# Channel taps computed during the start, half of unit 1's stores issued by GpSimd, and unit 2's conv jobs begun four steps earlier

## The chip, the cores and the metric

The kernel runs on one core of a Trainium2 chip. The metric is the device time of one execution in microseconds; the time before is the median of three runs, 773.52 us (773.24 to 773.58). A core has five engines that run side by side, each with an instruction queue of its own that is worked in order: TensorE (PE, matmuls; PEld are its weight loads), VectorE (DVE), ScalarE (ACT), GpSimd (POOL) and SyncE (SP, which here only issues DMAs). They wait for one another by semaphores. DMAs are issued by SyncE or by GpSimd and land later. GpSimd's DMAs can change the type on the way (float32 to float16), and SyncE's can transpose.

## What is computed

A lightweight convolution is followed by a gated feed-forward block. The reference, cut to what matters:

```python
# x: (8, 4096, 192), weight: (8 heads, 7 taps); 192 channels = 8 heads x 24
w = exp(weight - max) ; w = w / (sum(w) + 1e-9)          # softmax over the 7 taps
x_pad = concatenate([zeros(6 rows), x])                  # causal, for each sequence
out[b, s, head, :] = sum_k w[head, k] * x_pad[b, s + k, head, :]
x = out.reshape(32768, 192)                              # tokens
g = x @ w_gate ; val = x @ w_val                         # (192, 1536) each
result = (g / (1 + exp(-g)) * val) @ w_out               # (1536, 192), float32
```

## The kernel before

**Tiling.** The 32768 tokens are 64 blocks of 512 (`TB`), and four blocks make a unit (`UB`), so there are 16 units. A step `n` is one block and one of 12 slices of 128 hidden columns: 768 steps in all, `b, j = divmod(n, 12)`. In a step, `gate_val(n)` makes six matmuls of 512 columns (three slices of 64 channels, for gate and for val side by side, line 846), ScalarE the silu (L855) and VectorE the product `h` (L857). The down projection is done for three steps at a time: in each step with `j % 3 == 1`, `slot` and `down` issue 24 matmuls into the accumulators (L872), and its first one waits for the silu of two steps before. So the work has a period of three steps. When a block's sums are ready, ScalarE and VectorE copy them out (L929, L930) and SyncE stores them (L933). The order of the instructions on each engine is the order in which the code calls `seq`.

**Four ways to the convolved, transposed input.** Blocks 0 to 3 (unit 0) go through `early` or `early_pair`, matmuls with a banded matrix, and are transposed on TensorE by `eturn` (L490 the transposes, L501 the copies out of the bank) or, for block 3, through DRAM. Unit 1 (blocks 4 to 7) goes through `conv_half` (steps 25 and 31): matmuls L531, copies to `tm` (L548), one copy by GpSimd (`conv_dup`, L559), then nine stores to DRAM (`conv_out`, L567 and L575, all by SyncE, called at steps 31 and 32), then transposing loads (`fetch`, L589, three for each block, at steps 32, 35, 38 and 41). Units 2 to 15 (`POOLED`) are convolved element by element: GpSimd casts x into DRAM (`cast_x`, L649), SyncE loads it transposed (`turn_x`, L665) and joins a half tile to another (`join_x`, L669), and a conv job for each of six tiles of a unit multiplies by the seven channel taps: ScalarE tap 0 and two more (L742), VectorE two (L717), GpSimd two and the sums (L707, L692). `place` (L766) then puts the tiles together.

**What sets the order.** `planned(v)` gives the steps at which unit v's head, cast, turns, joins and jobs are called; `queue_jobs` puts six jobs into two lists (`act_steps`, `dve_steps`), and `pooled_work` takes from them one ScalarE and one VectorE piece in the steps with j = 1, 4, 7 and 10 (ScalarE; two in every other j = 10) and j = 1, 7 and 10 (VectorE). Unit 2's jobs are called at step 38, its first join at step 36.

**The channel taps.** A job needs, for each of 128 channels, the seven taps of its head (`both_taps`). They are made from the softmaxed weights `split` by a matmul with a 0/1 matrix of heads by channels (`pick`). GpSimd prepares `which` and `above` for it at the start (L210, L218, behind the loads of the weights), VectorE makes `pick` at step 34 (L609), and at step 37 TensorE makes four small matmuls (L620) into a gate bank and ScalarE copies them out (L627).

**The start.** GpSimd issues, in this order: block 0's x, the first third of gate and val weights (`load_w(0)`), the second third, block 1's x, the last third, `w_out` in thirds, and x for blocks 2 and 3 and for unit 1. Meanwhile the taps are spread to a banded matrix (`make_wide`, L344, with `ident` L352 for the transposes), then `early(0)` convolves block 0 (L386, copies L404 and L413), `eturn(0)` transposes it, and step 0 begins.

PSUM has three banks for gate, three for val and two accumulators; each new tile of a tag takes the next bank in turn and waits until the last reader of that bank is done.

## Time and profile before

| what | us or share |
|---|---|
| median of three runs | 773.52 (773.24 to 773.58) |
| the profiled execution: its own time | 772.68 |
| its span, and the rest around it | 770.9 and 1.8 |
| granted TensorE clock, mean over the span | 0.999 |
| step 0's first gate matmul starts | 8.78 |
| step 767's first gate matmul starts | 763.75 |
| a conv piece on ScalarE (L742), VectorE (L717), mean | 0.71, 1.07 |
| a sum on GpSimd (L692, total with part), mean | 1.28 |
| first conv piece on GpSimd starts, idle time ahead of it | 60.97, 20.6 |

The profile is of one execution. Busy shares say how much of the span an engine worked; the chain that ended last says which work the end of the run followed from; the list of waits says who waited for whom, and the timeline gives the instructions of a stretch in the order of time: start, duration, engine, line, operation, `out<-in`, shape, count, and in brackets the idle time of the engine before it with what ended it. Successive matmuls overlap, so that the pace is read from their starts, not from their durations. A row of several instructions ("x3") begins with the first of them and gives the time from its start to the last one's end.

### The profile page before, as it was taken

What the parts mean: (1) busy time and instruction counts of PE and PEld (TensorE: products, weight loads), DVE (VectorE), ACT (ScalarE), POOL (GpSimd) and SP (SyncE); (2) the same over time, 40 slices, a digit from 0 to 9 for tenths busy, and PEclk for the clock granted to TensorE, in tenths of its full rate; (3) what the DMA queues carried; (4) which work ended last, traced back from release to release, by engine and by line L of the source; (5) the groups of instructions that cost most, each with busy time, mean ns of one, the idle gap of its engine ahead of it and who ended that gap; (6) DMA issues with size and microseconds to landing.
All of it is one profiled execution on the core that took longest, in us unless ns stands there. A gap on an engine that the chain in (4) does not pass through costs nothing.

```text
span 770.9 us, 27696 instructions
## 1 busy us (share of the span) xinstructions
PE 764.5 (99%) x11041; PEld 673.9 (87%) x11041; DVE 697.3 (90%) x1042; ACT 645.1 (84%) x1107; POOL 618.1 (80%) x557
## 2 busy tenths in 40 slices
PE   8999999999999999999999999999999999999997
PEld 5766688888888888999999999999999999999997
DVE  7778999999999999999999999999999999999775
ACT  6678888888888888888888888888888888888664
POOL 9105889999989898998989989999899998889300
PEclk9999999999999999999999999999999999999999
DMA  9968746653545444456443444336454443221211
GB/s 138 190 131 136 143 77 154 128 87 90 117 85 125 102 86 106 99 99 116 85 107 93 93 118 108 92 84 116 92 118 100 84 116 90 55 67 40 70 57 43
DMA packets 140898, 77.78 MB, mean 101 GB/s; under 512 B 84632, under 2 KB 137632, under 8 KB 140768
## 3 DMA queue, kind: packets, MB, share of 16 engines
q1 hardware_dynamic: 127824, 60.24, 34.3%
q0 software_dynamic: 12944, 15.77, 13.4%
q8 instruction: 86, 1.41, 0.7%
q14 instruction: 44, 0.36, 0.2%
HBM read 31.54 MB, written 37.58 MB: 90 GB/s over the span
## 4 chain that ended last, share of the span: by engine, by line
PE 97%; SPq 1%; ACT 0%; DMA 0%; issue 0%; DVE 0%; ACTq 0%
PE gate L846 32%; PE val L846 32%; PE acc L872 31%; SPq L589 1%; PE warm L946 0%; PE turn L490 0%; SPq L567 0%; PE acc L893 0%; DMA x<-x 0%; PE cv L531 0%; PE cv L386 0%; PE cv L429 0%; ACT tme L404 0%; DVE h L857 0%; ACT wide L344 0%
## 5 line engine op out<-in xcount | busy, mean ns | idle before, releaser
L857 DVE TENSOR_TENSOR h<-sig,val 128x512 f16<-128x512 f16 x768 | 497.6, 683 | 65.5 <-PE gate L846 48.9
L855 ACT ACTIVATE sig<-gate 128x512 f16<-128x512 f32 x768 | 457.5, 597 | 110.4 <-PE gate L846 71.9
L846 PE MATMUL gate<-pxc,w 64*128 64x512 f16 x2016 | 471.2, 376 | 0.0
L846 PE MATMUL val<-pxc,w 64*128 64x512 f16 x2016 | 471.1, 376 | 0.0
L846 PEld LDWEIGHTS <-w 64*128 64x128 f16 x4608 | 397.4, 110 | 65.2 <-issue 1.1
L872 PE MATMUL acc<-wo,h 64*128 64x192 f16 x6096 | 319.2, 243 | 0.2
L872 PEld LDWEIGHTS <-h 64*128 64x128 f16 x6096 | 301.3, 94 | 19.3 <-ACT sig L855 1.1
L692 POOL TENSOR_TENSOR total<-total,part 128x512 f32<-128x512 f32 x168 | 214.1, 1275 | 70.3 <-DVE total L717 50.5
L717 DVE SCALAR_TENSOR_TENSOR total<-x,both_taps,total 128x512 f32<-128x512 f16 x168 | 179.4, 1068 | 0.0
L707 POOL TENSOR_SCALAR piece<-x,both_taps 128x512 f32<-128x512 f16 x168 | 154.5, 920 | 0.0
L692 POOL TENSOR_TENSOR total<-total,piece 128x512 f32<-128x512 f32 x84 | 119.1, 1417 | 7.0
L742 ACT ACTIVATE part<-x,both_taps 128x512 f32<-128x512 f16 x168 | 120.0, 715 | 0.0
L692 POOL TENSOR_TENSOR pxc<-total,piece 128x512 f16<-128x512 f32 x56 | 71.6, 1279 | 4.7
L846 PE MATMUL val<-xc,w 64*128 64x512 f16 x288 | 68.5, 376 | 0.0
L846 PE MATMUL gate<-xc,w 64*128 64x512 f16 x288 | 68.2, 377 | 0.0
L742 ACT ACTIVATE total<-x,both_taps 128x512 f32<-128x512 f16 x84 | 60.0, 714 | 1.2 <-DMA x<-x 1.2
L692 POOL TENSOR_TENSOR y<-total,piece 128x512 f16<-128x512 f32 x28 | 35.6, 1273 | 2.3
L930 DVE COPY o_sb<-acc 128x384 f32<-128x384 f32 x63 | 34.6, 549 | 0.0
L929 ACT COPY o_sb<-acc 128x384 f32<-128x384 f32 x63 | 29.7, 471 | 3.3 <-PE acc L872 3.3
L559 POOL COPY tm<-tm 128x1280 f16<-128x1280 f16 x1 | 1.3, 1251 | 17.4 <-DVE tm L548 17.4
L649 POOL DMA_DIRECT2D xs<-in_x_dram x14 | 8.5, 606 | 0.0
L946 PE MATMUL warm<-fill 128*128 128x512 f16 (+1 forms) x12 | 4.2, 510 | 1.0 <-DVE fill L92 1.0
(73 smaller groups left out, 65.1 us busy)
## 6 DMA issues: line engine op xcount, KB each, us to landing
out_dram<-o_sb SPq DMA_DIRECT2D x63, 384.0 KB
pxc<-pxc SPq DMA_DIRECT2D x112, 64.0 KB
pxc<-y SPq DMA_DIRECT2D x112, 64.0 KB
xs<-in_x_dram POOLq DMA_DIRECT2D x7, 774.0 KB, 6.8
xs<-in_x_dram POOLq DMA_DIRECT2D x7, 768.0 KB, 6.7
x<-in_x_dram POOLq DMA_DIRECT2D x4, 480.0 KB, 11.0
x<-x SPq DMA_DIRECT2D x28, 66.0 KB
x<-xs SPq DMA_TRANSPOSE x112
```

Of the source, the lines that this page charges most:

```text
L589: nc.sync.dma_start_transpose(out=t[:, 0:TB], in_=scr[u][TB * i : TB * i + TB, Q * k : Q * k + P])
L649: nc.gpsimd.dma_start(out=flat[skip * D : rows * D].rearrange("(a n) -> a n", n=n), in_=bass.AP(tensor=x_flat.tensor, offset=(u * UT - XP ...
L692: nc.gpsimd.tensor_tensor(job["dst"] if k == K - 1 else total, total, part, op=ALU.add)
L707: nc.gpsimd.tensor_scalar(part, shifted(k), scalar1=job["tap"][:, k : k + 1], scalar2=1.0, op0=ALU.mult, op1=ALU.mult,)
L717: nc.vector.scalar_tensor_tensor(job["total"], shifted(k), job["tap"][:, k : k + 1], job["total"], op0=ALU.mult, op1=ALU.add,)
L742: nc.scalar.activation(part, shifted(k), AF.Copy, scale=job["tap"][:, k : k + 1])
L846: nc.tensor.matmul(o, w16[m][p0 : p0 + Q, k, e::E], xc[b][k][p0 : p0 + Q, 0:TB], start=(k == 0), stop=(k == SL - 1),)
L855: silu[n] = seq(nc.scalar.activation(sg, g, AF.Silu)).ins
L857: seq(nc.vector.tensor_tensor(hj, sg, v, op=ALU.mult))
L872: nc.tensor.matmul(acc[b][bank][:, s, :], hj[p0 : p0 + Q, ts(2 * bank + s, P)], wo16[p0 : p0 + Q, j, :], start=(not second and j == 0 and ...
L929: seq(nc.scalar.copy(o_sb[:, 0:2, :], acc[b][0]))
L930: seq(nc.vector.tensor_copy(o_sb[:, 2:4, :], acc[b][1]))
```

## The change

The index rows that `pick` is made from become one row of head numbers (`head_of`), which GpSimd writes between the first and the second third of the weights; two such rows and two compares behind `w_out` go. `make_picks` now compares `head_of` with the partition number in one instruction for all 192 channels and one for the last 64 again, and is called between `make_wide` and `early(0)`. `make_channel_taps` is called inside `eturn(0)`, behind its transposes, and takes a val bank; the copy out (`copy_channel_taps`) is called behind `eturn(0)`'s copies. Of unit 1's eight numbered stores, 1, 3, 5 and 7 are issued by GpSimd; the ninth, the rest of store 7, stays with SyncE. Unit 2's first join moves from step 36 to step 32, where it follows block 4's three transposing loads and precedes block 5's; its jobs are called at step 34 instead of 38, so that the first ScalarE piece is in step 37 instead of 40. Otherwise the order on SyncE's queue stays as it was; on GpSimd's, unit 3's cast (called at step 56) comes behind the second conv job's pieces instead of ahead of them.

```diff
--- before.py
+++ after.py
@@ -196,26 +196,18 @@
     cid = small("cid", [P, P], i32)
     seq(nc.gpsimd.iota(cid, pattern=[[1, P]], base=0, channel_multiplier=0))
     load_w(0)
+    head_of = small("head_of", [H, D], i32)
+    seq(
+        nc.gpsimd.iota(
+            head_of, pattern=[[1, H], [0, grp]], base=0, channel_multiplier=0
+        )
+    )
     load_w(1)
     xe_tile(1)
     xe_load(1)
     load_w(2)
     for m in range(3):
         load_wo(m)
-    which = {}
-    above = {}
-    for name, first, rows in (("c01", 0, P), ("c2", P, Q)):
-        which[name] = small(f"which_{name}", [H, P], i32)
-        seq(
-            nc.gpsimd.iota(
-                which[name],
-                pattern=[[0, P // rows], [1, rows]],
-                base=first,
-                channel_multiplier=-grp,
-            )
-        )
-        above[name] = small(f"above_{name}", [H, P])
-        seq(nc.gpsimd.tensor_single_scalar(above[name], which[name], 0, op=ALU.is_ge))
     xp = cpool.tile([P, 2 * EG, D], fp16, tag="xp", name="xp", bufs=1)
     for r in range(2):
         windows(xp, Q * r, (2 + r) * TB, EO, 0, 2 * EG)
@@ -476,7 +468,7 @@
             )
             xc[b].append(t)
 
-    def eturn(b, where):
+    def eturn(b, where, then=None):
         tiles = [
             cpool.tile([P, XW], fp16, tag=f"xc{k}", name=f"xc{k}", bufs=8)
             for k in range(SL)
@@ -491,6 +483,8 @@
                         bank[:, g, :], tme[b][:, g, Q * k : Q * k + P], ident
                     )
                 )
+        if then is not None:
+            then()
         whole = ((dve, 0, 0, 0, 0, P), (act, 1, 0, 1, 0, P), (dve, 2, 0, 2, 0, P))
         halves = (
             (dve, 0, 0, 0, 0, P), (act, 2, 0, 2, 0, P),
@@ -508,6 +502,8 @@
                 )
             )
         xc[b] = tiles
+        if b == 0:
+            copy_channel_taps()
 
     tm = {}
     scr = {}
@@ -560,11 +556,12 @@
 
     def conv_out(u, m):
         r, c = divmod(m, 4)
+        queue = nc.gpsimd if m % 2 else nc.sync
         t0 = NG * CO * m
         full = min(NG, (UT - t0) // CO)
         rest = min(UT - t0 - full * CO, CO) if full < NG else 0
         seq(
-            nc.sync.dma_start(
+            queue.dma_start(
                 out=scr[u][t0 : t0 + full * CO, :].rearrange("(g j) d -> j g d", j=CO),
                 in_=tm[u][32 * c : 32 * c + CO, NG * r : NG * r + full, :],
             )
@@ -603,17 +600,21 @@
     pick = {}
 
     def make_picks():
-        for name in which:
-            pick[name] = small(f"pick_{name}", [H, P], fp16)
-            seq(
-                nc.vector.scalar_tensor_tensor(
-                    pick[name], which[name], float(grp), above[name],
-                    op0=ALU.is_lt, op1=ALU.mult,
-                )
-            )
+        picks = small("picks", [H, 2 * P], fp16)
+        for c0, c1, to in ((0, D, 0), (P, D, D)):
+            seq(
+                nc.vector.tensor_scalar(
+                    picks[:, to : to + c1 - c0], head_of[:, c0:c1], scalar1=pf[0:H],
+                    scalar2=None, op0=ALU.is_equal,
+                )
+            )
+        pick.update(c01=picks[:, 0:P], c2=picks[:, P : 2 * P])
+
+    tap_bank = []
 
     def make_channel_taps():
-        bank = ppool.tile([P, TB], fp32, tag="gate", name="ctap")
+        bank = ppool.tile([P, TB], fp32, tag="val", name="ctap")
+        tap_bank.append(bank)
         for m, name in enumerate(pick):
             for a in range(2):
                 seq(
@@ -623,8 +624,10 @@
                         skip_group_check=True,
                     )
                 )
+
+    def copy_channel_taps():
         both_taps = small("both_taps", [P, 2 * K])
-        seq(nc.scalar.copy(both_taps, bank[:, 0 : 2 * K]))
+        seq(nc.scalar.copy(both_taps, tap_bank[0][:, 0 : 2 * K]))
         for m, name in enumerate(pick):
             taps[name] = both_taps[:, m * K : m * K + K]
 
@@ -785,11 +788,11 @@
             (0, 0), (0, Q), (1, Q), (1, 0), None, (2, 0), (2, Q), (3, Q), (3, 0), None
         )
         if v == 2:
-            head, cast, jobs = 10, 21, 38
+            head, cast, jobs = 10, 21, 34
             turns = (
                 (0, 0), (0, Q), (1, Q), None, (1, 0), (2, 0), (2, Q), (3, Q), None, (3, 0)
             )
-            times = (24, 24, 24, 36, 36, 39, 39, 42, 42, 42)
+            times = (24, 24, 24, 32, 36, 39, 39, 42, 42, 42)
         elif v == 3:
             head, cast, jobs = 56, 56, 39
             times = range(66, 86, 2)
@@ -956,8 +959,9 @@
     spread_taps()
     keep_warm(4, 2 * P)
     make_wide()
+    make_picks()
     early(0, (gate_bank, gate_bank, val_bank))
-    eturn(0, (*acc_banks, gate_bank))
+    eturn(0, (*acc_banks, gate_bank), make_channel_taps)
     make_band()
     for v in POOLED:
         planned(v)
@@ -1000,10 +1004,6 @@
             eout(3)
         elif n == 19:
             efetch(3)
-        if n == 34:
-            make_picks()
-        if n == 37:
-            make_channel_taps()
         pooled_work(n, j, work is not None)
         if u + 1 < NU and not pooled(u + 1):
             if ls == at[0]:
```

## The prediction

> **What bounds the kernel now.** I read the engine totals first, then the chain of work that ended last, then the list of waits, and last the order of time on TensorE around the two places that the change touches. Totals and chain, from the page:

> ```profile
> PE 764.5 (99%) x11041; PEld 673.9 (87%) x11041; DVE 697.3 (90%) x1042; ACT 645.1 (84%) x1107; POOL 618.1 (80%) x557
> ...
> PE 97%; SPq 1%; ACT 0%; DMA 0%; issue 0%; DVE 0%; ACTq 0%
> ```

> TensorE (PE) is the path for 97% of the span; no other engine is on it except SyncE's queue (SPq) for 1%. So time is to be won only where TensorE does something it need not do, or stands still. A regular stretch of three steps takes 2.93 us: in the chain, the groups of 24 acc matmuls start at 67.92, 70.85, 73.78 and so on, 2.93 apart, up to the tail. The 255 stretches measured by the starts of their gate matmuls differ from 2.93 by more than 0.06 only in the first 35 steps and in two others. The first of the two, in the order of time on TensorE:

> ```profile
> 50.61 0.26 PE L620 MATMUL ctap<-split,pick_c 8*128 8x7 f16 x4
> 50.80 0.40 PE L846 MATMUL gate<-xc,w 64*128 64x512 f16 x1
> ```

> These are the channel taps of step 37. The stretch that ends at 50.80 began at 47.58 and took 3.22 us, 0.29 over the regular. The second:

> ```profile
> 64.29 0.38 PE L846 MATMUL gate<-xc,w 64*128 64x512 f16 x1
> 64.29 0.38 PE L846 MATMUL val<-xc,w 64*128 64x512 f16 x1
> 64.81 1.16 PE L872 MATMUL acc<-wo,h 64*128 64x192 f16 x24
> ```

> Gate pairs follow each other every 0.21 us, so acc was due at 64.50 and came at 64.81; the whole stretch (62.56 to 65.81) took 3.25, 0.32 over. The reason, in the order of time of the other engines:

> ```profile
> 52.87 8.54 SPq L589 DMA_TRANSPOSE xc<-scr  x6
> ...
> 61.45 0.60 SPq L669 DMA_DIRECT2D x<-x  x1
> ...
> 63.55 0.73 ACT L742 ACTIVATE total<-x,both_taps 128x512 f32<-128x512 f16 x1 [1.18 <-DMA x<-x]
> ...
> 64.18 1.55 ACT L855 ACTIVATE sig<-gate 128x512 f16<-128x512 f32 x3
> ```

> Unit 2's first join (L669) is issued at 61.45, behind six transposes, and lands 2.0 us later. ScalarE (ACT) asked for it at 62.37, waited 1.18, and behind this conv step stood the silu that the acc matmuls wait for. So 1.18 us of wait cost TensorE 0.32: some 0.86 us of such a wait is free.

> **The change part by part.** Sums are made against the profiled execution (772.68 us: span 770.9 and 1.8 around it). It lies 0.84 under the median of the runs shown (773.52), so I carry the difference over to the median.

> *Taps leave step 37.* Four matmuls and their weight loads go: -0.29 by the stretch above, which holds the rest of their cost too (a gate bank fewer in turn). The two picks on VectorE (DVE) and the copy on ScalarE (0.47 and 0.17 us) go as well, both from idle time: 0.

> *Taps enter the start.* The relevant rows:

> ```profile
> 6.60 0.28 DVE L352 TENSOR_SCALAR ident<-cid,pf 128x128 f16<-128x128 int32 x1
> ...
> 7.36 0.56 DVE L404 CAST tme<-cv 128x384 f16<-128x384 f32 x1 [0.48 <-PE cv L386]
> 7.78 1.04 PE L490 MATMUL turn<-ident,tme 128*128 128x128 f16 x15 [0.50 <-ACT tme L404]
> ...
> 8.30 0.99 DVE L501 COPY xc<-turn 128x520 f16<-128x520 f16 x2
> ...
> 8.57 0.59 ACT L501 COPY xc<-turn 128x520 f16<-128x520 f16 x1 [0.85 <-PE turn L490]
> 8.78 0.38 PE L846 MATMUL gate<-xc,w 64*128 64x512 f16 x1
> ```

> VectorE: two new compares stand in the 0.48 us of idle time ahead of 7.36. No row has their sizes; the same kind of work takes 0.28 for 128 elements (ident) and 0.41 for 256 (shift), so 0.35 for 192 and 0.21 for 64: 0.56. Without overlap they end at 6.88 + 0.56 = 7.44, 0.08 late; with the 0.08 by which instructions without a dependence overlap here (L311 ends at 5.24, L340 starts at 5.16) they end at about 7.28. Bounds 0 and +0.08; I take 0, since ident itself overlapped its forerunner. What is late behind them, should they be late, is the cast, the turn and the first gate, one for one.

> TensorE: four tap matmuls now stand between the last transpose (start 8.60) and the first gate (8.78). At step 37 they started at 50.61 and let gate in at 50.80, 0.19; behind 8.66 that makes the first gate some 8.87. But the second pair waits for ScalarE's copy and starts at 9.22 anyway; the first needs 0.21 before it, so it may start as late as 9.01. Bounds 0 and, at the whole 0.29, 8.66 + 0.29 + 0.21 - 9.22, less than nothing: 0. ScalarE's tap copy (0.17) goes in behind its copy, which ends at 9.16, and the first silu starts at 9.84 after 0.68 of idle time: 0. The bank is the third val bank, not used before; the val matmul that needs it next is that of step 2 (10.29).

> GpSimd (POOL): an index row goes in ahead of the load of the second weights (issued at 5.53). Nearest rows: 0.18 from the start of cid's to the next issue, 0.32 from a which row to the next instruction; I take 0.25. Behind it are queued w1, block 1's x, w2 and wo. The transfers run on with a backlog: the DMA share is 1.13 to 1.27 in each two us from 6 to 14, and landing takes 5.0 to 6.0 us from issue where the first weights took 3.5 to 3.9. So a delay of 0.25 in the queue's filling should be eaten by it. Cover gone: block 1's x (issued at 7.90, 6.0 to landing: 13.92) is needed at 13.98, so up to 0.28 would fall on the path. Bounds 0 and +0.28; I take 0. Four instructions behind wo (12.83 to 14.46) go, so later loads are issued up to 1.6 us earlier into the same backlog: 0.

> *Four stores by GpSimd.* The nine stores took SyncE from 46.36 to 52.87, 0.72 each; four leave, 2.9 us, so its first transpose could be issued at 50.0. On GpSimd they cost 0.54 to 0.87 each (its other issues), some 2.8 us from 45, and it idles from 40.3 to 61.0: 0. Nothing is queued behind them but the first conv job (start 60.97, now some 3 us sooner). The first transposes now need GpSimd's first store too: it can be issued when ScalarE's casts end (44.97), and transfers of its size by GpSimd landed in 3.5 to 6.0, median 5.3 (weights): 48.5 to 51.0, so the transposes start at 50.0 to 51.0; I take 50.3.

> [...]

> *Join ahead of block 5, jobs from step 34.* The join stands behind three transposes instead of six: 50.3 + 4.66 (52.87 to 57.53) = 55.0, and 2.0 to land: 57.0 (57.7 at the late bound). ScalarE now asks one slot of three steps earlier: 62.37 - 2.93 - 0.29 = 59.15. Margin 1.5 to 2.1, and 0.86 more before TensorE feels it: -0.32, all of it. Block 5's transposes move behind one join (0.6), and are some 2 us earlier nonetheless. The other jobs keep their spacing, each a slot earlier; unit 2's second join and SyncE move by about the same (3.2 and 2.9). GpSimd's load of unit 3 (67.60) goes behind one more job, about 7 us later; its transposes stood at 85.11 in SyncE's queue, when it had landed for 9.6 us: 0.

> Sum: -0.29 - 0.32 + 0 = -0.61, that is 772.07 for the profiled execution and **772.9 us** for the median.

> **The rivals.**
> (1) *The start takes part of it back.* Picks +0.08 and block 1's x +0.28, both at their bound: -0.61 + 0.36 = -0.25, 773.3. For it: 0.06 us between landing and use. Against: the backlog.
> (2) *The wait on the join comes back*, or goes to unit 2's second join, 0.3 long: only the taps are won, 773.2. For it: jobs ask 2.93 sooner, and SyncE wins only 2.9. Against: the reorder puts the join 3.9 us further ahead.
> (3) *Slower: GpSimd's first store lands late.* Block 4's first gate is due at 60.28 - 0.29 = 59.99; its transposes take 4.6 from their start and some 2.0 to land. So it decides from a landing at 53.4, 8.4 us behind the issue, and from there costs one for one. Four x loads and a cast took up to 14.7 and 16.3 so: at 14.7, 44.97 + 14.7 + 6.6 = 66.3, 6.3 late, 773.52 - 0.29 + 6.3 = 779.5. Against: those stood in a full queue (DMA share 1.35 from 15 to 37; 0.68 from 44 to 50), and GpSimd's queue is empty since 37.4.
> (4) *The change does nothing on the path*: what the two stretches lose appears elsewhere, 773.5.

> **How the numbers follow.** Forecast 0.65; (1) 0.12; (2) 0.09; (3) 0.05; (4) 0.03; 0.06 for what I don't see, half to each side. A measurement of this kernel tells some 0.2% (1.55 us) from no change. Forecast, (1), (2) and (4) are all within: 0.89. Faster than 771.97 only the unseen and an occasion that runs low: 0.05. Slower than 775.07: (3) and some unseen, 0.06. Range: the profiled execution shows that one occasion can lie 0.84 under others, so 772.9 less 0.8, 772.1; above, no change at all and the runs' own 0.3: 773.8.

> **What would show it.** In the changed profile: no stretch over 2.96 behind step 37; no wait of ScalarE on the join; the taps' four matmuls between 8.6 and 8.9, with the second gate pair still at 9.2; GpSimd's first store issued at 45 and block 4's first transpose at 50 to 51. Wrong would make it: a first gate pair after 9.0, block 1's early conv later than 14.0, or a transpose on SyncE that starts after 53.

## The result, and the profile after

The changed kernel takes 775.44 us (median of 20 runs, 772.99 to 779.62) where the kernel before takes 773.19 on the same chip (20 runs, 772.65 to 777.50): a ratio of 1.0032, with a 95% interval of 1.0019 to 1.0045 (taken over all the runs, so it is not quite the quotient of the medians). Forecast were 772.9 and no measurable change; it is slower, by 2.2 us, and the median lies above the range. The profiled execution took 774.76 us with a span of 773.0, 2.1 more than before, so it is a fair sample to look for the loss in, though it lies 0.7 under the median of its kernel.

The totals and the chain that ended last, from the page of the changed kernel:

```profile
PE 764.2 (99%) x11041; PEld 605.6 (78%) x11041; DVE 697.6 (90%) x1042; ACT 644.9 (83%) x1107; POOL 620.1 (80%) x558
...
PE 96%; DMA 2%; POOL 1%; SPq 1%; ACT 0%; issue 0%; ACTq 0%; POOLq 0%
```

TensorE has as much work as before (764.2 against 764.5), but a share of the chain has gone to DMA and GpSimd: the end waited for transfers somewhere. (GpSimd's 1% and nearly half of the DMA's 2% lie in the first 12 us, where weights are loaded.) The list of waits (us in total, times, longest) says where:

```profile
PE val L849 <- DMA w<-in_moe_w_val_dram: 0.4, 1, 0.4
...
ACT total L745 <- DMA x<-x: 3.6, 2, 2.9
...
PE acc L875 <- ACT sig L858: 1.8, 1, 1.8
```

(Some lines stand three further down here: gate and val L849, acc L875, silu L858, ScalarE's conv steps L745, the join L672, the transposes of unit 2 L668, the cast L652.) TensorE waited once for ScalarE, and ScalarE twice for a join, 2.9 us the longer time. The stretches of three steps, measured by the starts of their gate matmuls, place it. Step 0 to step 767 took 756.98 us after 754.97 before, 2.01 more:

| stretch from step | before | after | difference |
|---|---|---|---|
| 0 to 2 | 1.52 | 1.36 | -0.16 |
| 2 (start) | 2.03 | 2.70 | +0.67 |
| 35 (taps at step 37) | 3.22 | 2.93 | -0.29 |
| 50 (unit 2's first join) | 3.25 | 2.93 | -0.32 |
| 71 (unit 2's second join) | 2.93 | 4.95 | +2.02 |
| 77 | 2.93 | 3.07 | +0.14 |

So both gains that were forecast came, to the hundredth, and a new stall of 2.0 us at the second join, where before nothing waited, took them and more. The order of time around it, on TensorE (start, duration, engine, line, operation, `out<-in`, shape, count, idle time with what ended it):

```profile
84.78 0.38 PE L849 MATMUL val<-xc,w 64*128 64x512 f16 x1
87.00 1.16 PE L875 MATMUL acc<-wo,h 64*128 64x192 f16 x24 [1.85 <-ACT sig L858]
```

and on the other engines:

```profile
76.91 1.29 SPq L668 DMA_TRANSPOSE x<-xs  x1
...
77.29 0.64 POOL L652 DMA_DIRECT2D xs<-in_x_dram  x1
...
83.75 0.47 SPq L672 DMA_DIRECT2D x<-x  x1
...
85.74 0.72 ACT L745 ACTIVATE total<-x,both_taps 128x512 f32<-128x512 f16 x1 [2.89 <-DMA x<-x]
86.37 1.55 ACT L858 ACTIVATE sig<-gate 128x512 f16<-128x512 f32 x3
```

Before, the same instructions stood so:

```profile
67.60 0.62 POOL L649 DMA_DIRECT2D xs<-in_x_dram  x1
...
78.62 1.26 SPq L665 DMA_TRANSPOSE x<-xs  x1
...
81.61 0.47 SPq L669 DMA_DIRECT2D x<-x  x1
...
86.04 0.71 ACT L742 ACTIVATE total<-x,both_taps 128x512 f32<-128x512 f16 x1
```

To read: ScalarE now asks for the second join's data at 82.85 (85.74 less 2.89) instead of 86.04. SyncE issues the transpose ahead of the join 1.7 us sooner than before (76.91 against 78.62), yet the join 2.1 us later (83.75 against 81.61): the wait between the two grew from 1.7 to 5.5 us. What SyncE waited for is the transpose, and the chain that ended last runs through it and the join (start, duration, what):

```profile
76.91 6.82 DMA x<-xs
83.75 1.91 DMA x<-x
```

In between, GpSimd's load of unit 3 (`cast_x`, 774 KB) has moved from 67.60 to 77.29, behind the second conv job's pieces, as the prediction said; and the DMA engines, between 79.5 and 82 us of the changed kernel, are all but its alone (queue, kind: packets, MB, share of 16 engines' time; q0 is GpSimd's, q1 SyncE's):

```profile
q0 software_dynamic: 142, 0.44, 102.8%
q1 hardware_dynamic: 11, 0.00, 0.6%
```

The transpose's data packets (256 B) stop at 79.5 to 80, but its packets of 4 B come only between 82.1 and 83.4 and its 16 reports of landing between 82.7 and 83.73, while the cast's 256 packets of 3096 B, 0.25 us each (median), 16 to a DMA engine on average, go through (started 78.8 to 83.8). Until then the join is not issued.

### The profile page after: what moved, and what is told of

The parts are those of the page before. It is cut to its first block, busy times and chain, and to the rows that moved or that the text cites. A ratio compares the mean times of both kernels' runs of the same rounds, so it can differ in the third digit from the quotient of the medians.

```text
span 773.0 us, 27698 instructions
## 1 busy us (share of the span) xinstructions
PE 764.2 (99%) x11041; PEld 605.6 (78%) x11041; DVE 697.6 (90%) x1042; ACT 644.9 (83%) x1107; POOL 620.1 (80%) x558
## 4 chain that ended last, share of the span: by engine, by line
PE 96%; DMA 2%; POOL 1%; SPq 1%; ACT 0%; issue 0%; ACTq 0%; POOLq 0%
PE val L849 47%; PE acc L875 32%; PE gate L849 16%; DMA x<-xs 1%; DMA w<-in_moe_w_val_dram 1%; SPq L586 1%; POOL w L168 0%; POOL xe L98 0%; PE acc L896 0%; DMA x<-x 0%; PE turn L482 0%; PE cv L527 0%; PE cv L421 0%; ACT part L745 0%; PE cv L378 0%
## 5 line engine op out<-in xcount | busy, mean ns | idle before, releaser
L858 ACT ACTIVATE sig<-gate 128x512 f16<-128x512 f32 x768 | 457.2, 597 | 110.7 <-PE gate L849 75.1
L849 PE MATMUL gate<-pxc,w 64*128 64x512 f16 x2016 | 471.2, 376 | 0.0
L849 PE MATMUL val<-pxc,w 64*128 64x512 f16 x2016 | 471.1, 376 | 0.0
L849 PEld LDWEIGHTS <-w 64*128 64x128 f16 x4608 | 349.6, 110 | 127.9 <-DMA w<-in_moe_w_val_dram 1.1
L875 PE MATMUL acc<-wo,h 64*128 64x192 f16 x6096 | 334.0, 243 | 1.9 <-ACT sig L858 1.8
L875 PEld LDWEIGHTS <-h 64*128 64x128 f16 x6096 | 307.2, 94 | 27.1 <-ACT sig L858 3.0
L745 ACT ACTIVATE part<-x,both_taps 128x512 f32<-128x512 f16 x168 | 117.2, 714 | 0.0
L849 PE MATMUL val<-xc,w 64*128 64x512 f16 x288 | 68.2, 376 | 0.4 <-DMA w<-in_moe_w_val_dram 0.4
L849 PE MATMUL gate<-xc,w 64*128 64x512 f16 x288 | 68.4, 377 | 0.0
L745 ACT ACTIVATE total<-x,both_taps 128x512 f32<-128x512 f16 x84 | 60.1, 715 | 3.6 <-DMA x<-x 3.6
L652 POOL DMA_DIRECT2D xs<-in_x_dram x14 | 8.5, 604 | 0.0
L564 POOL DMA_DIRECT2D scr<-tm x4 | 2.6, 650 | 5.3 <-ACT tm L544 5.3
## 6 DMA issues: line engine op xcount, KB each, us to landing
xs<-in_x_dram POOLq DMA_DIRECT2D x7, 774.0 KB, 7.5
```

The costliest lines, as they stand in the source:

```text
L652: nc.gpsimd.dma_start(out=flat[skip * D : rows * D].rearrange("(a n) -> a n", n=n), in_=bass.AP(tensor=x_flat.tensor, offset=(u * UT - XP ...
L745: nc.scalar.activation(part, shifted(k), AF.Copy, scale=job["tap"][:, k : k + 1])
L849: nc.tensor.matmul(o, w16[m][p0 : p0 + Q, k, e::E], xc[b][k][p0 : p0 + Q, 0:TB], start=(k == 0), stop=(k == SL - 1),)
L858: silu[n] = seq(nc.scalar.activation(sg, g, AF.Silu)).ins
L875: nc.tensor.matmul(acc[b][bank][:, s, :], hj[p0 : p0 + Q, ts(2 * bank + s, P)], wo16[p0 : p0 + Q, j, :], start=(not second and j == 0 and ...
```

## Experiments

Each kernel ran 12 times beside the kernel before. "Cast" is unit 3's load by GpSimd, "join" unit 2's second join unless it says first.

### 1 to 4: the cast's place, the jobs' step, the stores, the taps

Four kernels change one thing of the changed kernel each. *e1_cast54* issues the cast ahead of the second conv job's pieces again; *e2_jobs38* puts the conv jobs back to step 38; *e3_stores_sp* gives all stores back to SyncE; *e4_old_taps* has the taps where they were, with the rest of the change.

```diff
# e1_cast54
-            head, cast, jobs = 56, 56, 39
+            head, cast, jobs = 54, 54, 39
# e2_jobs38
-            head, cast, jobs = 10, 21, 34
+            head, cast, jobs = 10, 21, 38
# e3_stores_sp
-        queue = nc.gpsimd if m % 2 else nc.sync
+        queue = nc.sync
# e4_old_taps: the kernel before, with
+        queue = nc.gpsimd if m % 2 else nc.sync
-            head, cast, jobs = 10, 21, 38
+            head, cast, jobs = 10, 21, 34
-            times = (24, 24, 24, 36, 36, 39, 39, 42, 42, 42)
+            times = (24, 24, 24, 32, 36, 39, 39, 42, 42, 42)
```

> The changed kernel with one edit: unit 3's cast (GpSimd, 768 KB) is called at step 54 instead of 56, so that in GpSimd's queue it stands ahead of the second conv job's pieces, as before the change. Theory (the cast's packets hold up the transpose that unit 2's second join waits for): the cast is issued near 68 and has landed by 77, the join is issued at 80 or sooner, ScalarE's wait of 2.9 us on it and TensorE's 2.0 us behind it are gone; median 772.7 to 773.3. Rival A (jobs ask three steps too early, SyncE's queue can't follow): the join is as late as in the changed kernel, some 83.7, and the median stays at 775 or more. Rival B (the start: the index row ahead of the second weights delays them): the 2 us are in the first 20 us and stay; 775 or more.

> The changed kernel with unit 2's jobs called at step 38 again instead of 34; stores, join and taps as changed. The cast then stands ahead of the second job's pieces by itself, and jobs ask 2.9 us later. Theory (cast): 772.6 to 773.2, no wait on either join. Rival A (jobs ask too early): the same here; this run alone can't part the two, the run with the cast at step 54 does. Rival B (start): 775 or more.

> The changed kernel with all nine stores by SyncE again. Theory (cast): SyncE's queue is 1.5 to 3 us later, the transpose ahead of the second join is issued still more into the cast's packets, the wait is as long or longer: 775.5 to 778. Rival C (GpSimd's stores are what costs, by the weight of their packets or by making the transposes wait): back to 773 or less.

> The kernel before with stores, join and jobs of the change, but with its channel taps where they were (index rows behind w_out, picks at step 34, matmuls at step 37). Theory (cast): the second join waits as in the changed kernel, and step 37 costs its 0.29 again: 775.2 to 776.2. Rival B (start): with nothing put ahead of the second weights the loss is gone, 772.9 to 773.5.

| kernel | median (range) | before, beside it | ratio (95%) |
|---|---|---|---|
| e1_cast54 | 773.37 (772.31 to 778.00) | 773.15 | 1.0003 (0.9985 to 1.0021) |
| e2_jobs38 | 772.50 (772.12 to 773.00) | 773.15 | 0.9986 (0.9976 to 0.9996) |
| e3_stores_sp | 775.20 (774.10 to 777.70) | 773.15 | 1.0026 (1.0013 to 1.0040) |
| e4_old_taps | 775.15 (772.69 to 777.65) | 773.15 | 1.0015 (0.9997 to 1.0033) |

In e1 the cast is out of the way (issued 67.74, landed 75.26), and the 2.0 us are gone; from the order of time of e1:

```profile
67.74 0.64 POOL L652 DMA_DIRECT2D xs<-in_x_dram  x1
...
81.07 0.47 SPq L672 DMA_DIRECT2D x<-x  x1
...
83.18 0.72 ACT L745 ACTIVATE total<-x,both_taps 128x512 f32<-128x512 f16 x1 [0.58 <-DMA x<-x]
```

No stretch of e1's profile behind step 32 is over 2.96, and step 2 to step 767 takes 752.82, 0.63 less than before. But the margin is thin: ScalarE still waits 0.58 us (harmless, by the 0.86 us that the profile of before showed to be free), and 4 of 12 runs lie above 774 (what held them up is not shown), so the median is not better than before. The join itself comes only 0.5 us sooner than before (81.07 against 81.61), while ScalarE asks 3.4 sooner (82.60 against 86.04).

In e2 the cast is early too, since its place is counted in conv jobs (67.31); ScalarE waits for no transfer at all, and step 2 to step 767 takes 752.85, 0.60 less than before: the sum of the prediction, 0.61, to 0.01. Its interval lies wholly under 1: it is faster than the kernel before, by 0.1%.

e3 has the cast late (77.66) and SyncE's stores back. The join is issued early there, at 79.38, and still its data come late:

```profile
77.66 0.64 POOL L652 DMA_DIRECT2D xs<-in_x_dram  x1
...
79.38 0.47 SPq L672 DMA_DIRECT2D x<-x  x1
...
86.64 0.72 ACT L745 ACTIVATE total<-x,both_taps 128x512 f32<-128x512 f16 x1 [3.41 <-DMA x<-x]
```

Here it is the copy of 66 KB that stands behind the cast's packets: its own first packet starts 3.7 us after the issue, where e1's starts after 1.1. From issue to use it took some 7 us, where e1's took 2.1, but not all of that is the cast's. The copy's packets were through at 84.2, and 14 of its 16 reports of completion arrived only at 86.3 and later. Packets that started at 84.6 took up to 1.73 us there, where 0.04 is usual, while 16 KB of instructions were being loaded (84.27 to 85.54). Some 1.7 of the 3.41 us are this second hold-up. The changed kernel has none at its join, whose last report came 1.9 us after the issue. The stores are not what made the change slower: e3, without any on GpSimd, is as slow. And after this stall the granted clock fell; busy time of the engines in two windows of e3 (us; then the clock, the DMA share and GB/s):

```profile
84.00:88.00 4.00, 1.63 (x20) 0.68 (x16) 0.85 (x2) 1.36 (x3) 3.84 (x4) 1.00 1.18 210
88.00:92.00 4.00, 4.00 (x38) 2.45 (x37) 3.35 (x5) 2.02 (x4) 3.83 (x5) 0.57 0.73 146
```

The stretch with the stall took 6.06 us, 3.13 over, and the next, at half clock for 3.41 us, another 1.09 over.

In e4 the cast is issued at 78.19, the join at 78.58, just behind it; ScalarE waited 1.04 us, TensorE 0.18 over. The stretch of step 35 keeps its 0.29 there: the taps' old place costs just that. Its runs scatter over 5 us, and the interval holds no change.

### 5 and 6: jobs at step 38 with the cast late, and without GpSimd's stores

```diff
# e5_jobs38_cast59
-            head, cast, jobs = 10, 21, 34
+            head, cast, jobs = 10, 21, 38
-            head, cast, jobs = 56, 56, 39
+            head, cast, jobs = 59, 59, 39
# e6_jobs38_stores_sp
-            head, cast, jobs = 10, 21, 34
+            head, cast, jobs = 10, 21, 38
-        queue = nc.gpsimd if m % 2 else nc.sync
+        queue = nc.sync
```

> The changed kernel with jobs from step 38 and unit 3's cast called at step 59, behind the second job's pieces: the fourth corner of jobs (34, 38) by cast (ahead, behind). GpSimd reaches the cast near 80, so its packets run from about 81.5 to 86.5, over the second join's own copy (issued near 81.5 in the run with jobs from 38); ScalarE asks for it near 85. Theory (nothing of SyncE's moves while the cast's packets run): the copy lands near 87, ScalarE waits 1 to 2 us, TensorE loses 0.2 to 1.2: 772.7 to 774.0, with a wait on a join that the run with the cast ahead doesn't have. Rival A (early jobs alone are the cause): no wait, 772.5.

> The fast version (jobs from step 38) with all nine stores by SyncE. By the prediction's step (four stores fewer free SyncE for 2.9 us) the first transpose of block 4 would start near 55 to 56 and the first join land near 61 to 62, still in time or all but: 772.5 to 772.8. Rival (the stores' pace on SyncE is set by their packets, not by their issue, so that moving four to GpSimd frees nothing): first transpose at 52 to 53, join issued at 57 to 58 as with GpSimd's stores, 772.5.

e5 took 772.75 us (772.14 to 774.35; before 773.20; ratio 0.9986, 0.9969 to 1.0003): a late cast with late jobs costs nothing. I had expected a wait of 1 to 2 us there, which did not come. Its order of time says why:

```profile
78.43 0.47 SPq L672 DMA_DIRECT2D x<-x  x1
...
79.32 0.64 POOL L652 DMA_DIRECT2D xs<-in_x_dram  x1
```

The join was ahead of the cast, by 0.9 us, and its packets were through at about 80, before the cast's began at 80.8. So late is not what hurts: it is the cast's place between the transpose and the join's data. (No run has the jobs at 38 and the cast in that place.) Together with the runs above: (jobs 34, cast early) 773.37, (34, late) 775.44, (38, early) 772.50, (38, late) 772.75. In these runs neither edit alone costs anything; the jobs' step 34 makes ScalarE ask early, and the cast, moved by it, holds the join up.

e6 took 772.38 us (772.08 to 772.88; before 773.20; ratio 0.9969, 0.9952 to 0.9987), the lowest median of all, without a store on GpSimd. What the stores on GpSimd free in SyncE's queue is seen in these two rows, the first of e2 (with them):

```profile
47.31 5.45 SPq L564 DMA_DIRECT2D scr<-tm  x4
```

and the second of e6 (without):

```profile
47.26 5.88 SPq L564 DMA_DIRECT2D scr<-tm  x8
```

Four stores took SyncE nearly as long there as eight (over the twelve profiles four took 3.69 to 5.76 us, eight 5.54 to 5.88). The first transpose of block 4 starts at 53.33 in e2 and 53.91 in e6; over all kernels it lies between 51.80 and 55.14, and 51.80 is e3, which has none on GpSimd.

### 7 and 9: a smaller packet, a cast in four parts

Both have the jobs at 34 and the cast late, as the changed kernel. *e7_small_cast* cuts the cast's packets to a quarter (774 B, 64 to a DMA engine on average); *e9_cast_in_4* issues it as four transfers of 193.5 KB, with packets as before.

```diff
# e7_small_cast
-                max_dma_last_dim=8192,
+                max_dma_last_dim=2048 if u == 3 else 8192,
# e9_cast_in_4 (in cast_x)
+        parts = 4 if u == 3 else 1
+        e = (rows - skip) * D // parts
+        for part in range(parts):
+            o = skip * D + part * e
...
-                out=flat[skip * D : rows * D].rearrange("(a n) -> a n", n=n),
+                    out=flat[o : o + e].rearrange("(a n) -> a n", n=n),
...
-                    ap=[[n, P], [1, n]],
+                        ap=[[n, P // parts], [1, n]],
```

> The changed kernel (jobs from step 34, cast behind the second job's pieces) with unit 3's cast cut into 1024 rows of 387 elements instead of 256 of 1548: the same bytes in packets of 774 B instead of 3096. Theory as it stands (SyncE's packets stand still until the cast's are through): two variants are parted. If it is the size of a packet that shuts the others out, SyncE's packets now get between, the second join lands near 81 to 82, and the time falls to 772.5 to 773.8. If it is the cast's place in the queue of the DMA engines, the wait stays: 775 to 776. Rival A (early jobs): 775 to 776 too, with the join late though its packets move.

> The changed kernel (jobs from step 34, cast behind the second job's pieces) with unit 3's cast in four DMAs of 64 rows each instead of one of 256, so that each of the 16 DMA engines gets four lots of four transfers instead of one of 16. Theory with a turn-taking of whole lots (a DMA engine takes one lot to its end, then turns to SyncE's queue): SyncE's completions and the join get between after one lot, about 1 us, the second join lands by 82 to 83 and the wait mostly goes: 772.5 to 774.0. Theory with first come, first served (whatever the cast has queued goes first): the wait of 2 to 4 us stays, 775 to 776.5. GpSimd pays three more issues of some 0.6 us either way.

Neither took the wait away. e7 took 776.02 us (772.25 to 779.66; before 773.20; ratio 1.0022, 0.9998 to 1.0046); ScalarE waited 4.21 us for a join issued at 80.10. e9 took 774.65 (772.30 to 776.47; before 773.08; ratio 1.0007, 0.9987 to 1.0027), and in its order of time:

```profile
77.25 2.14 POOL L656 DMA_DIRECT2D xs<-in_x_dram  x4
...
79.06 0.47 SPq L676 DMA_DIRECT2D x<-x  x1
...
86.32 0.72 ACT L749 ACTIVATE total<-x,both_taps 128x512 f32<-128x512 f16 x1 [3.51 <-DMA x<-x]
```

The join was issued 1.8 us behind the cast's first part, and between 79.5 and 82 us not one packet of SyncE's queue went through; the queues of e9 in that window, all of them:

```profile
q0 software_dynamic: 197, 0.51, 107.7%
```

The join's packets (1056 B) ran between 82.5 and 84.1. The one cast of the changed kernel has 16 packets to a DMA engine on average, and 11 packets of SyncE's ran beside it from 79.5 to 82; the four parts of e9 have 4 each, and beside them none ran. Turn-taking by such parts, which was to let the join get between after about 1 us, was thus not seen. The wait of 3.51 us lies in the 2 to 4 expected with first come, first served, the median of 774.65 between the two forecasts, so that these runs do not decide in what order a DMA engine takes the packets of two queues. What they show is that neither smaller packets nor more transfers let the join's data in much sooner: its packets started at 83.27 (e7) and 82.47 (e9), after 83.10 in e3. Why the transpose's 4 B packets come so late in the changed kernel (82.1 to 83.4, its data by 80), no run isolates.

What the order does is shown by a table over eight kernels (issue times in us; in the kernel before, e6, e8 and e10 the cast stands at 67 to 69, as in e2, and ScalarE does not wait for the second join either):

| kernel | cast | second join | join behind the cast's issue by | ScalarE waits for it |
|---|---|---|---|---|
| e2_jobs38 | 67.31 | 81.52 | 14.2 | 0 |
| e1_cast54 | 67.74 | 81.07 | 13.3 | 0.58 |
| changed kernel | 77.29 | 83.75 | 6.5 | 2.89 |
| e7_small_cast | 77.23 | 80.10 | 2.9 | 4.21 |
| e9_cast_in_4 | 77.25 | 79.06 | 1.8 | 3.51 |
| e3_stores_sp | 77.66 | 79.38 | 1.7 | 3.41 |
| e4_old_taps | 78.19 | 78.58 | 0.4 | 1.04 |
| e5_jobs38_cast59 | 79.32 | 78.43 | -0.9 | 0 |

Where the cast had landed (75 us) or came behind the join, there is little wait or none; wherever it stands just ahead, there is one, whatever else differs among these five, which all have the jobs at 34. The size of the wait does not follow the order alone: e7 and e9 have the hold-up of e3 at 84 to 86 us too, and in e4 the join's data had landed at 84.7, just before it.

### 8 and 10: the taps alone, the join alone

```diff
# e8_taps_only: the changed kernel, with
-        queue = nc.gpsimd if m % 2 else nc.sync
+        queue = nc.sync
-            head, cast, jobs = 10, 21, 34
+            head, cast, jobs = 10, 21, 38
-            times = (24, 24, 24, 32, 36, 39, 39, 42, 42, 42)
+            times = (24, 24, 24, 36, 36, 39, 39, 42, 42, 42)
# e10_join_only: the kernel before, with
-            times = (24, 24, 24, 36, 36, 39, 39, 42, 42, 42)
+            times = (24, 24, 24, 32, 36, 39, 39, 42, 42, 42)
```

> The changed kernel with stores by SyncE, the first join behind block 5's transposes and jobs from step 38, as before the change: the channel taps at the start are all that is left of it. Theory (prediction's first term): the stretch of step 37 falls from 3.22 to 2.93 us, the stretch of the first join stays at 3.25 or so, and the second pair of gate matmuls starts as before: -0.29, 772.8 to 773.0. Rival B (the index row ahead of the second weights costs the start): waits on weights within the first 20 us in most looks, 773.2 or more.

> The kernel before with one edit: unit 2's first join at step 32, behind block 4's transposes and ahead of block 5's. Taps, stores and jobs as before. Theory (prediction's second term): ScalarE's wait on the first join is gone, the stretch of step 50 falls from 3.25 to 2.93 and step 37's stays at 3.22: 772.7 to 773.0 by the profile, and the runs above 774, which the kernel before has in one of five, go too if they came from that wait. Rival: they stay, as the second join has them too.

e8 took 774.41 us (772.63 to 777.72; before 773.20; ratio 1.0008, 0.9990 to 1.0027). Its stretch of step 35 is regular, so the taps' 0.29 are won; but the median is above the 772.8 to 773.0 that I expected. The first join, still behind six transposes, comes at 62.59 there:

```profile
53.34 9.20 SPq L586 DMA_TRANSPOSE xc<-scr  x6
62.59 0.60 SPq L672 DMA_DIRECT2D x<-x  x1
...
65.93 0.72 ACT L745 ACTIVATE total<-x,both_taps 128x512 f32<-128x512 f16 x1 [3.85 <-DMA x<-x]
```

TensorE stood still for 2.8 us, the stretch of step 50 took 2.98 over. This profile lies above the median of its runs; it shows how long the wait on the first join can be, 1.18 us in the profile of before. Here too 15 of the join's 16 reports had arrived at 64.62 and the last at 65.84, beside a load of 16 KB of instructions (63.44 to 64.63). In the profile of before the join had landed at 63.47, just as such a load began (63.40).

e10 took 772.95 us (772.17 to 773.81; before 773.08; ratio 0.9986, 0.9969 to 1.0002). Its stretch of step 50 is regular (the 0.32 are won by the join's place alone), that of step 35 keeps its 0.29. Its profile lost 0.29 at another place, to a wait of 0.78 us on a transpose at 78.95 (e6 has the like, 0.74 us at 77.49, for 0.25). Of its 12 runs none is above 774; of those of the kernel before, 2 of 20, 4 of 35, 11 of 35 and 5 of 22 are. In e2 and e6, which have the join ahead of block 5 as well and the jobs at 38, none of 24 is. So the earlier join also seems to take away the long runs; no long run of the kernel before was profiled, so that this is a reading of the spread and not shown.

## Why the prediction was wrong

*Taps leave step 37, -0.29:* right. The stretch is 2.93 in every kernel with the new place, and 3.22 in those with the old one (e4, e10).

*Taps enter the start, 0:* right in what it said of TensorE. Block 0's turn started at 7.41 (before 7.78), the tap matmuls 0.97 behind it, the second gate 1.44 behind it in both. From the order of time on TensorE of the changed kernel:

```profile
8.38 0.26 PE L621 MATMUL ctap<-split,picks 8*128 8x7 f16 x4
8.57 0.40 PE L849 MATMUL gate<-xc,w 64*128 64x512 f16 x1
...
12.16 0.41 PE L849 MATMUL val<-xc,w 64*128 64x512 f16 x1 [0.45 <-DMA w<-in_moe_w_val_dram]
```

The wait at 12.16, for a part of the second weights, is the 0.67 of the table (by the starts, 0.82 us lie between this matmul and the one before it, where 0.21 is regular). The index row stands ahead of that load (issued at 6.32 instead of 6.13), but is not the cause: this part landed at 12.12 there, and in the other eight kernels with the row between 10.88 and 11.76, against 11.46, 11.69 and 11.97 in the three without. It scatters by more than the row costs. The prediction's sign that block 1's early convolution starts after 14.0 was met by this (14.23).

*Four stores by GpSimd, SyncE 2.9 us sooner:* wrong, and without harm. The step took 0.72 us per store as SyncE's own cost of issuing. In the changed kernel:

```profile
47.93 4.58 SPq L564 DMA_DIRECT2D scr<-tm  x4
52.56 0.80 SPq L572 DMA_DIRECT2D scr<-tm  x1
53.81 4.15 SPq L586 DMA_TRANSPOSE xc<-scr  x3
58.01 0.60 SPq L672 DMA_DIRECT2D x<-x  x1
```

Five stores took 5.4 us, 1.09 each, and the transposes started at 53.81, not at 50.3. That the issuing engine does not set the pace is shown by e2 and e6, where four stores and eight took 5.45 and 5.88 us. The likely reason is that all stores need the same DMA engines, which were busy for 0.84 of the time from 48 to 54 us here; no run isolates it. The prediction's own sign of error (a transpose of block 4 later than 53) was met. GpSimd's stores were issued at 45.88 in 0.64 us each, so that the rival of a late first store did not occur.

*Join ahead of block 5, -0.32:* right in the sum, wrong in the margin. The join came at 58.01 instead of 55.0, ScalarE waited 0.74 us (at 60.13) and 0.86 were free, so that the full 0.32 came with some luck. In two other kernels with jobs at 34 it waited 0.98 (e7, where the stretch of step 47 took 0.11 over) and 0.59 (e9). The place of the join carries it alone (e10). The 0.86 us themselves, worked out from one row, held: the wait less 0.86 is the stretch's loss in the changed kernel (2.89, 2.02), in e4 (1.04, 0.18), in e8 (3.85, 2.98) and in e7's second join (4.21, 3.34).

*"Unit 2's second join and SyncE move by about the same (3.2 and 2.9)", and "GpSimd's load of unit 3 (67.60) goes behind one more job, about 7 us later; its transposes stood at 85.11 in SyncE's queue, when it had landed for 9.6 us: 0":* these are the steps that failed. The load moved by 9.7 us, and the question put to it was only who waits for its data: nobody did. Not asked was what its packets stand in front of. They stood before the report of the transpose that the second join waits for (in e3 before the join's own data), and this cost 2.0 us in the profile. The first half fails by itself too: without the cast in the way (e1) the second join moved by 0.5 us, not 2.9, and its margin was 0.6 short.

*Rivals.* (1) Steps 0 to 5 took 4.06 us after 3.55 before, 0.5 more, but by the weights' landing just named and neither by the picks (they ended on time) nor by block 1's x. (2) had the place, "or goes to unit 2's second join", and the wrong size: 0.3 there, 2.0 in the profile. Why many runs are longer still than the profiled one is not fully shown. Nine of the 20 lie at 777.2 or above, all with a mean clock of 0.995 to 0.997, and the other eleven, up to 775.55, have 0.999 or 1.000. A mean of 0.997 is that of the profiles of e3, e7 and e9, each with one stretch of 3.41 us at half clock. So a stall after which the clock falls, as in e3 with its loss of 4.2 us in two stretches, would make such runs; but none of the nine was profiled.

## What to carry to other kernels

When a job list is moved, its transfers move too (the cast by 9.7 us here), and a large one has two customers: whoever waits for its data, and whatever another queue has to move while it passes (102.8% of the DMA engines' time from 79.5 to 82 us was the cast's, 0.6% SyncE's); look at both. A wait that vanishes at one place lets the work behind it ask sooner, so its next transfer has to be shown to come sooner by as much (in e1 ScalarE asked 3.4 us sooner, the join came 0.5 us sooner). And an issue time in a busy queue need not be the issuing engine's own cost: the same row with half the stores tells which (5.45 us for four in e2, 5.88 for eight in e6).

## What the runs showed of the hardware

A transfer of GpSimd of 774 KB held SyncE's queue off for some 2 to 3 us: in the changed kernel 102.8% of the DMA engines' time from 79.5 to 82 was its own (in e3 97.1% from 80 to 84, beside 3.5% of SyncE's), and the first packet of a copy of 66 KB behind it started 3.7 us after the issue (e3) against 1.1 (e1).

The second hold-up, beside a load of 16 KB of instructions, is in all the profiles. Between 20 and 760 us the twelve have 182 stretches in which five packets or more of at most 1.1 KB took over 0.9 us each; 181 of them begin within such a load or its neighbourhood (0.3 us ahead of it to 0.8 us behind), though these cover only a quarter of the time (12 of 12 in the kernel before and 17 of 17 in the changed one, where they cover 24% and 25%). Why, and why most loads pass without one, no run shows.

TensorE's clock fell to half for 3.41 us after standing still for 2.4 us (e3), 2.5 (e9) and 3.2 (e7), and this cost 1.6 to 1.7 us beyond the wait less 0.86 (in e3, a loss of 4.21 in two stretches for a wait of 3.41); after 1.85 us (changed kernel) and after 2.8 us (e8) it stayed. The two windows of e8, as those of e3 above:

```profile
64.00:68.00 4.00, 1.19 (x24) 0.82 (x22) 0.84 (x2) 2.07 (x5) 3.78 (x4) 1.00 0.46 87
68.00:72.00 4.00, 4.00 (x62) 2.66 (x58) 3.85 (x7) 3.47 (x8) 0.00 (x0) 1.00 0.97 148
```
